# Both halves of P V in one step, one pair of PSUM buffers for four users, and logits scaled as they are copied

## The chip, the core and the metric

The kernel runs on one core of a Trainium2 chip. The metric is device time in microseconds (us) of one execution. TensorE (PE, with its weight loads PEld) multiplies matrices into PSUM; VectorE (DVE), ScalarE (ACT) and GpSimd (POOL) work on PSUM and SBUF; SyncE (SP) issues the DMAs, transposes by DMA among them, in one queue.

## What is computed

The reference chains three layers over batches of 576 positions and 512 channels:

```python
# 1. attention in a window of 64 positions, 8 heads of 64
scores = scale * np.matmul(q, k.transpose(0, 1, 3, 2))
mask = (rel >= 0) & (rel < window)
attn = softmax(np.where(mask, scores, -1000000000.0))
x = np.matmul(attn, v)                       # heads side by side: 512 channels
# 2. gated convolution over 5 positions
gate = 1.0 / (1.0 + np.exp(-gate_pre))       # gate_pre: causal convolution of x
x = gate * (x @ w_val) @ w_out
# 3. four causal attention experts, the best two of each position
logits = x @ w_gate
q, k, v = x @ wq[e], x @ wk[e], x @ wv[e]
ye = softmax(causal(scale * (q @ k.T))) @ v @ wo[e]
out = sum of w[e] * ye over the two experts with the largest logits
```

All eight batches use the same weights; results are float32.

## The kernel before

A batch is cut into five tiles of 128 positions (j = 0 to 4, the last of 64), so there are 40 tiles, numbered 0 to 39. Each goes through the same stages. In the first attention: raw q and k are loaded and transposed on TensorE (qt, L669) into PSUM tile tr and copied out (kT, qT); scores (sp, L726 to L730) go to PSUM tile sc; maximum (L737), exponential (L744), a high and a low half-precision part of P (Phl, the low one is the residual of L282); a DMA transpose makes PT (L765); PV (L794) writes PSUM tile o; VectorE scales the row sums (rc, L799), takes the reciprocal (L802) and writes xn (L809). Then xn is transposed (xt, L829) into tr again and drained to xT and xs; TensorE multiplies with w_val (val, L890 to L892, PSUM pj), VectorE applies the gate (L898) and splits into gs; TensorE makes q and k of the experts (qk, L923 to L925) and v with the logits (v3, L941). VectorE does the routing (L992 to L1030). Scores of the experts (s3, L1073, PSUM sc), softmax, a transpose by DMA (P3T, L1118), y (L1153, PSUM o, drained to ys), the output projection (L1178 to L1180, PSUM pj) and the store follow. Products of full precision are made of three half-precision ones.

Matmuls come in several shapes of the array: 128x128 for most, 128x64 for PV of tiles 1 to 4 of a batch and for y, 64-row ones for scores. PV of a tile comes in two halves of four heads each, two planner operations of 24 matmuls (12 for the first tile of a batch, 24 in one operation for the last). Each half needs the PSUM tile o, which has a single buffer and which y uses too. The tile tr, also with a single buffer, is shared by the raw transposes (two a tile), the xn transposes, a transpose of the batch's scales, and some transposes of weights at the start.

No loop fixes the order of instructions. Every stage of every tile is handed to a planner (`Plan`) with a priority (start of the tile plus `OFF` of its stage), durations, what it reads and writes, and the buffers that it holds (`KIND` names the pool, `BUFS` its number of buffers). `Plan.order` starts operations one after the other by its own table of costs and the buffers that are free; the program is written in that order, so each engine has one fixed sequence. At the start the weights are loaded, converted, multiplied together (w_out with the experts' weights, L471 to L489) and split into wval and wproj, with filler matmuls (L1201) between. The lines that matter here:

```python
KIND = dict(..., o1=("o", 2), xp=("tr", 1), yp=("o", 1), qp=("tr", 2), scp=("tr", 1), ...)
for h in range(NB):                      # NB: 2 halves, 1 for the last tile
    op("pv", n, ..., lambda h=h: pv(h), r=[("PT", n)] + vr, w=[("o1", n, h)])
    chain("xn", n, ("rc", n, h), [rcs, rci], [("o1", n, h)], [])
    op("xn", n, ..., xn(h), ...)
```

Of the kernel before, what the change touches and what calls it, by code (L numbers as in the profile page):

```python
# [22 lines left out]
NEG1 = -1.0e37  # L23
PS = 4096.0

BUFS = dict(raw=5, rv=10, qT=2, kT=2, VA=4, VB=2, Phl=1, PT=1, xn=1, xT=3, xs=2, acc=2, ctmp=2, gs=5,
           P3hl=2, P3T=3, V3=7, q3=3, k3=2, ys=2, ot=1, am=2, scs=3, w4=3, sc=2, o=1, tr=1, pj=2,
           w64=3, t1=3, wbig=1, ab=4, wp=1, wcat=1)
KIND = dict(wf=("pj", 1), kT=("kT", 1), k3=("k3", 1), qp=("tr", 2), s1p=("sc", 1), s3p=("sc", 2), o1=("o", 2), xp=("tr", 1), yp=("o", 1),
            scp=("tr", 1), pv=("pj", 1), pq=("pj", 1), pw=("pj", 1), po=("pj", 1), P3hl=("P3hl", 2),  # L30
            P3T=("P3T", 2), wt=("tr", 2), wj=("pj", 2), wc=("sc", 1), wp=("wp", 0), cq=("wp", 0), wcat=("wcat", 0),
            ck=("wcat", 0), cv=("w64", 1))
II = 14109.34
STRETCH = 1.5
OFF = dict(yh=61969.4, x3=76298.1, vl=20442.0, vs=13922.2, qk=54953.8, val=50000.0, ot=20813.6, yn=88307.5, gv=18491.1,
           qt=454.3, qe=-25419.0, gl=26778.7, rt=99733.5, yl=94279.8, s3=67381.4, ex=47180.1, vh=31559.9, st=81376.7,
           xT=10029.4, dq=13818.2, xl=67807.4, am=-5435.3, ph3=58596.7, xn=-25423.0, v3h=38686.3,
           pl=23451.7, o=98000.0, ph=101124.6, pl3=67418.4, h3=52915.4, yt=64737.1, th=53943.5,
           v3l=14936.7, xt=4442.6, l3=40133.4, m3=74450.1, P3T=76142.0, sp=15925.6, ld=59750.6, pv=28118.3,
           vb=7408.6, cv=66570.7)  # L40
SMALL = 70.0
SYNC = dict(PE=200.0, DVE=150.0, ACT=150.0, POOL=100.0, SP=0.0, TQ=0.0, AQ=0.0)
AHEAD = 600.0
# [2 lines left out]
STQ = ("SP",)  # L46
VBQ = ("SP",)
C3Q = ("SP",)
WATV = 23439.39
WATP = 61184.73  # L50
DMA_A = 650.0
DMA_T = 850.0
TCOST = 60.0
QUEUE = 2500.0
BOOST = {0: 49596.2, 3: 463.2, 4: -4467.5, 5: 1761.0, 7: -1392.4, 8: 4527.3}
LD0 = -175524.04
LD1 = 1628.22
ORDER = "raw0 wv0 wv3 wv2 v2 v1 v3 v0 v4 wv1 cw wo2 raw1 wo wo1 raw2 wo0 raw3 wcat raw4 wo3".split()
TENG = "SP"
SWITCH = 93.0  # L60
COLD = 3400.0
# [5 lines left out]
TAIL = 2000.0  # L67
ABSX = -500.0
FILL = 36
EARLY = 2.85  # L70
BIAS = dict(DVE=1500.0, POOL=0.0, ACT=500.0)


# [144 lines left out]
def attention_conv_moe(ctx: ExitStack, tc: tile.TileContext, q, k, v, w_val, conv_w, w_out,  # L218
# [29 lines left out]
    def bank(key, shape, dtype=F32):  # L248
        return new(key, shape, dtype, psum, KIND[key[0]][0])

# [404 lines left out]
    def col(b, i):  # L655
        return T_["sc_d", b][:, i:i + 1]

    def attn1(n):
# [121 lines left out]

        def pv(half):
            pt = T_["PT", n]
            o = bank(("o1", n, half), [128, 4, 66])
            for i in range(4):
                if last:
                    g = ((slice(64 * r, 64 * r + 64), i, 2 * (i % 2 + 2 * (i // 2 ^ r)) + i // 2, T_["VB", n]) for r in (0, 1))
                elif j:
                    g = ((slice(64 * r, 64 * r + 64), 4 * half + i, 2 * i + half, va if r else T_["VB", n]) for r in (0, 1))
                else:
                    g = ((slice(0, 128), 4 * half + i, 2 * i + half, va),)  # L790
                g = tuple(g)
                for a, c in ((0, 0), (0, 1), (1, 0)):
                    for qs, hh, h, vt in g:
                        pe.matmul(o[qs, i, 0:65], lhsT=pt[:, a, hh, qs], rhs=vt[:, c, h, 0:65], start=a + c == 0, stop=a == 1)  # L794
# [14 lines left out]
            ve.tensor_mul(dst, o[:, :, 0:64], rc[:, :, None].to_broadcast([128, 4, 64]))  # L809

        vr = [("VA", n, 0), ("VA", n, 1)] + ([("VB", n)] if j else [])
        for h in range(NB):
            op("pv", n, (("PE", (18 if j else 13) * mm(65)),), lambda h=h: pv(h), r=[("PT", n)] + vr, w=[("o1", n, h)])
            chain("xn", n, ("rc", n, h), [("DVE", lambda h=h: rcs(h)), ("DVE", lambda h=h: rci(h))], [("o1", n, h)], [])
            op("xn", n, (("DVE", dv(256)),), lambda h=h: xn(h),
               r=[("o1", n, h), ("rc", n, h, 1)] + ([("xn", n, 0)] if h else []), w=[("xn", n, h)])
# [93 lines left out]
    def proj(n):  # L910
# [66 lines left out]

        def lg(e):
            w4 = new(("w4", n), [128, 8, E], F32, late())
            copy(e, w4[:, 0], T_["pw", n][:, 128:132])  # L980
        op("v3h", n, both(256, False), v3h,
           r=[("pw", n)], w=[("V3", n, 0)])
        op("v3l", n, (("DVE", dv(256)),), v3l, r=[("pw", n), ("V3", n, 0)], w=[("V3", n, 1)])
        op("v3l", n, both(4, False), lg, r=[("pw", n)], w=[("w4", n, 0)])

        def rtA():

            w4, p = T_["w4", n], T_["pw", n]
            r, raw = rr(), p[:, 128:132]
            other = w4[:, 0][:, None, :].to_broadcast([128, E, E])  # L990
            own = raw[:, :, None].to_broadcast([128, E, E])
            ve.tensor_tensor(r[:, :, 1], other, own, op=OP.is_equal)  # L992
            ve.tensor_tensor(r[:, :, 0], other, own, op=OP.is_gt)
            t = w4[:, 3]
            ve.tensor_reduce(t[:, 0:1], w4[:, 0], axis=AX.X, op=OP.max, negate=True)
            ve.tensor_scalar(t[:, 0:1], t[:, 0:1], col(b, 3), None, op0=OP.mult)

        def rr():
            return T_["pw", n][:, 288:320].rearrange("p (e i f) -> p e i f", e=E, i=2)
# [5 lines left out]

        def rtC():
            w4 = T_["w4", n]
            ac.activation(w4[:, 1], w4[:, 0], AF.Exp, bias=w4[:, 3, 0:1], scale=col(b, 3))

        def rtF():  # L1010
            w4 = T_["w4", n]
# [16 lines left out]
        def rtI():  # L1028
            w4 = T_["w4", n]
            ve.tensor_scalar(w4[:, 4], T_["pw", n][:, 264:268], w4[:, 3, 2:3], None, op0=OP.mult)  # L1030
        op("rt", n, (("DVE", 450.0),), rtA, r=[("pw", n), ("w4", n, 0), ("scs", b, 3)], w=[("pw", n, "c"), ("w4", n, 1)])
        op("rt", n, (("ACT", 190.0),), rtC, r=[("w4", n, 1)], w=[("w4", n, 2)])
        op("rt", n, (("DVE", 300.0),), rtB, r=[("pw", n, "c")], w=[("pw", n, "s")])
        op("rt", n, (("DVE", 250.0),), rtF, r=[("pw", n, "s"), ("w4", n, 2)], w=[("w4", n, 3)])
# [5 lines left out]
    def attn2(n):  # L1040
# [99 lines left out]

        def y():

            o = bank(("yp", n), [128, 2, 128])
            for c in range(2):
                for kt in range(nt):
                    K = rows(kt)
                    v3 = V3[(n0 + kt) % len(V3)]
                    for a, d in ((0, 0), (0, 1), (1, 0)):
                        for r in (0, 1):
                            e = 2 * c + r  # L1150
                            g, x = [(g, es.index(e)) for g, es in enumerate(groups) if e in es][0]
                            i, qs = (kt, slice(64 * x, 64 * x + 64)) if last else (x * nt + kt, slice(0, 128))
                            pe.matmul(o[64 * r:64 * r + 64, c, :T], lhsT=v3[:K, d, e], rhs=T_["P3T", n, g][:K, a * wt // 128 + i, qs],  # L1153
                                      start=c + kt + a + d == 0, stop=c == 1 and kt == j and a == 1)
# [1 line left out]
           [("V3", m, i) for m in range(n0, n + 1) for i in (0, 1)], w=[("yp", n)])  # L1156

        def yh(e):
            copy(e, new(("ys", n), [128, 2, 2, 128], F16, late())[:, 0, :, :T], T_["yp", n][:, :, :T], 1.0 / PS)
        op("yh", n, both(2 * T, False), yh, r=[("yp", n)], w=[("ys", n, 0)])  # L1160

        def yl():
            ys = T_["ys", n]
            residual(ys[:, 1, :, :T], T_["yp", n][:, :, :T], ys[:, 0, :, :T], 1.0 / PS)
        op("yl", n, (("DVE", dv(2 * T)),), yl, r=[("yp", n), ("ys", n, 0)], w=[("ys", n, 1)])

        def o_():
# [70 lines left out]
```

## Time and profile before

| | before |
|---|---|
| device time, median of 3 runs (lowest to highest) | 679.75 us (679.58 to 681.16) |
| device time of the profiled execution | 679.55 us |
| its span, first to last instruction | 677.7 us |
| TensorE busy | 628.5 us (93%) |
| VectorE busy | 557.4 us (82%) |
| ScalarE busy | 515.6 us (76%) |
| GpSimd busy | 483.1 us (71%) |
| mean granted TensorE clock | 0.985 |

The profiled execution and the median of the three runs differ by 0.2 us. "Busy" is the time that an engine executes; matmuls overlap in the array, so a busy TensorE can still lose time between two starts. [...] A wait in the trace is a stretch in which an engine stood still, with the work that ended it.

### The profile page before, as it was taken

To read this page: it belongs to the slowest core of one execution; us is meant where nothing else is said; L and a number is where in the kernel's file an instruction comes from. 1 tells how busy PE (TensorE), PEld (TensorE's weight loads), DVE (VectorE), ACT (ScalarE), POOL (GpSimd) and SP (SyncE) were. 2 spreads that over 40 slices of the span, in tenths; PEclk is the share of its full clock that TensorE was granted. 3 is DMA by queue.
4 is the path that set the end of the run, shared out by engine and by line. 5 is a ranking of instruction groups with operands and counts; after the bars stand their busy time and mean duration, and the time that the engine had idled before them with its cause. 6 is when DMAs were issued, how large, how long until landed. Compare 5 with 4: busy or idle time off the path is not lost. (4 is left out here: it accounts for less than half of the span.)

```text
span 677.7 us, 25338 instructions
## 1 busy us (share of the span) xinstructions
PE 628.5 (93%) x10225; PEld 489.9 (72%) x10237; DVE 557.4 (82%) x1695; ACT 515.6 (76%) x1340; POOL 483.1 (71%) x546
## 2 busy tenths in 40 slices
PE   8979979889999999999989999999999999999985
PEld 4436768677787778777877778777887688767753
DVE  7695697788979988998888886989789898887782
ACT  2656557877897888888797869787897888777773
POOL 4674967997596688786985879497977777973500
PEclk9989989999999999999999999999999999999998
DMA  8769952795995988967996977797686664556257
GB/s 224 188 164 194 235 114 46 163 168 107 157 223 120 173 153 139 196 129 143 162 184 142 180 134 154 156 177 150 114 172 129 96 127 111 98 114 118 43 123 145
DMA packets 306531, 99.45 MB, mean 147 GB/s; under 512 B 294362, under 2 KB 296942, under 8 KB 306414
## 3 DMA queue, kind: packets, MB, share of 16 engines
q1 hardware_dynamic: 306414, 97.84, 74.1%
q8 instruction: 80, 1.31, 0.8%
q14 instruction: 37, 0.30, 0.1%
HBM read 34.63 MB, written 9.44 MB: 65 GB/s over the span
## 5 line engine op out<-in xcount | busy, mean ns | idle before, releaser
L872 POOL TENSOR_TENSOR acc<-acc,ctmp 128x512 f32<-128x512 f32 (+1 forms) x160 | 185.9, 1162 | 6.3
L870 POOL TENSOR_TENSOR ctmp<-xT,cw 128x512 f32<-128x512 f32 (+1 forms) x160 | 151.5, 968 | 0.0
L744 ACT ACTIVATE sc<-sc,mx 128x128 f32<-128x128 f32 x288 | 99.0, 344 | 33.0 <-DVE mx L737 25.0
L890 PE MATMUL pj<-xs,wval 128*128 128x128 f16 (+1 forms) x640 | 101.1, 216 | 1.0 <-ACT k L275 1.0
L923 PE MATMUL pj<-gs,wproj 128*128 128x128 f16 (+1 forms) x640 | 101.6, 216 | 0.1
L924 PE MATMUL pj<-gs,wproj 128*128 128x128 f16 (+1 forms) x640 | 101.4, 216 | 0.0
L925 PE MATMUL pj<-gs,wproj 128*128 128x128 f16 (+1 forms) x640 | 101.4, 216 | 0.0
L891 PE MATMUL pj<-xs,wval 128*128 128x128 f16 (+1 forms) x640 | 101.0, 215 | 0.0
L892 PE MATMUL pj<-xs,wval 128*128 128x128 f16 (+1 forms) x640 | 100.9, 215 | 0.0
L1087 ACT ACTIVATE sc<-sc,mx 128x128 f32<-128x128 f32 (+3 forms) x144 | 75.9, 527 | 30.2 <-DVE mx L1082 27.3
L861 POOL TENSOR_TENSOR acc<-xT,cw 128x512 f32<-128x512 f32 (+1 forms) x31 | 31.7, 1023 | 81.9 <-issue 40.7
L282 DVE SCALAR_TENSOR_TENSOR P3hl<-sc,mx,P3hl 128x128 f16<-128x128 f32 (+3 forms) x144 | 75.8, 573 | 11.6 <-ACT P3hl L275 10.3
L275 ACT ACTIVATE P3hl<-sc,mx 128x256 f16<-128x256 f32 (+4 forms) x134 | 66.4, 564 | 8.9 <-DVE mx L1100 4.9
L1073 PE MATMUL sc<-k,q 64*128 64x128 f32 (+5 forms) x384 | 66.5, 451 | 4.9 <-DVE P3hl L282 3.5
L1082 DVE TENSOR_REDUCE mx<-sc 128x4 f32<-128x512 f32 (+3 forms) x64 | 61.5, 965 | 3.4 <-PE sc L1073 2.6
L923 PEld LDWEIGHTS <-wproj 128*128 128x128 f16 x640 | 62.1, 99 | 2.3 <-issue 0.5
L890 PEld LDWEIGHTS <-wval 128*128 128x128 f16 x640 | 61.9, 99 | 1.7 <-issue 0.9
L891 PEld LDWEIGHTS <-wval 128*128 128x128 f16 x640 | 61.9, 99 | 1.6 <-issue 1.1
L924 PEld LDWEIGHTS <-wproj 128*128 128x128 f16 x640 | 62.1, 99 | 0.5 <-issue 0.3
L925 PEld LDWEIGHTS <-wproj 128*128 128x128 f16 x640 | 62.1, 99 | 0.0
L892 PEld LDWEIGHTS <-wval 128*128 128x128 f16 x640 | 61.9, 99 | 0.0
L691 POOL TENSOR_TENSOR VA<-rv,VA 128x512 f16<-128x512 f32 (+1 forms) x40 | 45.9, 1156 | 19.5 <-ACT VA L275 11.4
(200 smaller groups left out, 1763.4 us busy)
## 6 DMA issues: line engine op xcount, KB each, us to landing
VB<-VA SPq DMA_DIRECT2D x64, 132.0 KB, 2.9
raw<-in_q SPq DMA_DIRECT2D x32, 256.0 KB, 3.9
raw<-in_k SPq DMA_DIRECT2D x32, 256.0 KB, 3.8
rv<-in_v SPq DMA_DIRECT2D x32, 256.0 KB, 3.9
out<-ot SPq DMA_DIRECT2D x32, 256.0 KB, 2.7
w<-in_moe_w_val SPq DMA_DIRECT2D x4, 512.0 KB, 5.2
w<-in_moe_w_out SPq DMA_DIRECT2D x4, 512.0 KB, 3.7
rv<-in_v SPq DMA_DIRECT2D x8, 128.0 KB, 3.5
```

The lines of the kernel that those rows point to most:

```text
L282: ve.scalar_tensor_tensor(o, i, scale, hi, op0=OP.mult, op1=OP.subtract)
L744: ac.activation(ps[:, i, :], ps[:, i, :], AF.Exp, bias=t[:, hh:hh + 1])
L870: po.tensor_mul(y, x[:, :, t + i:t + i + T], W["cw"][:, :, t + i:t + i + 1].to_broadcast([128, 4, T]))
L872: po.tensor_add(acc[:, :, :T], acc[:, :, :T], y)
L890: pe.matmul(p[:, m, :T], lhsT=w0, rhs=xs[:, 0, c, :T], start=c == 0, stop=False)
L891: pe.matmul(p[:, m, :T], lhsT=w0, rhs=xs[:, 1, c, :T], start=False, stop=False)
L892: pe.matmul(p[:, m, :T], lhsT=w1, rhs=xs[:, 0, c, :T], start=False, stop=c == 3)
L923: pe.matmul(p[:, m, :T], lhsT=w0, rhs=gs[:, 0, c, :T], start=c == 0, stop=False)
L924: pe.matmul(p[:, m, :T], lhsT=w0, rhs=gs[:, 1, c, :T], start=False, stop=False)
L925: pe.matmul(p[:, m, :T], lhsT=w1, rhs=gs[:, 0, c, :T], start=False, stop=c == 3)
L1073: pe.matmul(ps[ot, c0:c0 + r.shape[-1]], lhsT=l, rhs=r, start=bk not in seen, stop=i == final[bk])
L1087: ac.activation(ps[:, x], ps[:, x], AF.Exp, bias=mx[:, x:x + 1], accum_out=mx[:, 4 + x:5 + x])
```

## The change

PV of both halves becomes one planner operation, so that its 48 matmuls (24 for the first tile of a batch) stand in a row; the chains of rc and xn follow for both halves. Its two results, y, the raw and xn transposes and the transpose of the scales all use the PSUM tile tr, which now has two buffers; the tile o is gone. The PSUM tiles of PV and y are declared as large as a buffer and used in part. The copy of the logits out of PSUM multiplies them by the batch's scale, so that the maximum needs no scaling of its own and the exponential no scale; the two compares of the routing scale the other operand as they read it. xn gets a second buffer, v's raw tile rv nine instead of ten. The planner's tables (priorities, order of loads, and constants) have new values throughout, so the order changes on all engines.

```diff
-BUFS = dict(raw=5, rv=10, ..., xn=1, ..., sc=2, o=1, tr=1, pj=2,
+BUFS = dict(raw=5, rv=9, ..., xn=2, ..., sc=2, tr=2, pj=2,
-KIND = dict(..., o1=("o", 2), xp=("tr", 1), yp=("o", 1),
+KIND = dict(..., o1=("tr", 2), xp=("tr", 1), yp=("tr", 1),
-OFF = dict(yh=61969.4, x3=76298.1, vl=20442.0, vs=13922.2, qk=54953.8, val=50000.0, ot=20813.6, yn=88307.5, gv=18491.1,
+OFF = dict(yh=34829.2, x3=87092.4, vl=19158.9, vs=12206.5, qk=54953.8, val=50000.0, ot=19786.5, yn=88113.8, gv=18985.3,
...
-ORDER = "raw0 wv0 wv3 wv2 v2 v1 v3 v0 v4 wv1 cw wo2 raw1 wo wo1 raw2 wo0 raw3 wcat raw4 wo3".split()
+ORDER = "wv0 wv2 wv3 v4 raw0 v1 v3 v2 wv1 raw1 wo2 cw v0 raw2 wo3 raw3 wo wo1 wcat wo0 raw4".split()
...
-            o = bank(("o1", n, half), [128, 4, 66])
+            o = bank(("o1", n, half), [128, 512])[:, 0:264].rearrange("p (i d) -> p i d", d=66)
+            T_["o1", n, half] = o
...
+        def pvs():
+            for h in range(NB):
+                pv(h)
+        op("pv", n, (("PE", (18 if j else 13) * mm(65) * NB),), pvs, r=[("PT", n)] + vr, w=[("o1", n, h) for h in range(NB)])
         for h in range(NB):
-            op("pv", n, (("PE", (18 if j else 13) * mm(65)),), lambda h=h: pv(h), r=[("PT", n)] + vr, w=[("o1", n, h)])
...
-            copy(e, w4[:, 0], T_["pw", n][:, 128:132])
+            copy(e, w4[:, 0], T_["pw", n][:, 128:132], col(b, 3))
...
-            ve.tensor_tensor(r[:, :, 1], other, own, op=OP.is_equal)
-            ve.tensor_tensor(r[:, :, 0], other, own, op=OP.is_gt)
-            t = w4[:, 3]
-            ve.tensor_reduce(t[:, 0:1], w4[:, 0], axis=AX.X, op=OP.max, negate=True)
-            ve.tensor_scalar(t[:, 0:1], t[:, 0:1], col(b, 3), None, op0=OP.mult)
+
+            ve.scalar_tensor_tensor(r[:, :, 1], own, col(b, 3), other, op0=OP.mult, op1=OP.is_equal)
+            ve.scalar_tensor_tensor(r[:, :, 0], own, col(b, 3), other, op0=OP.mult, op1=OP.is_lt)
+            ve.tensor_reduce(w4[:, 3, 0:1], w4[:, 0], axis=AX.X, op=OP.max, negate=True)
...
-            ac.activation(w4[:, 1], w4[:, 0], AF.Exp, bias=w4[:, 3, 0:1], scale=col(b, 3))
+            ac.activation(w4[:, 1], w4[:, 0], AF.Exp, bias=w4[:, 3, 0:1])
...
-            o = bank(("yp", n), [128, 2, 128])
+            o = bank(("yp", n), [128, 4, 128])
```

How the order moves shows at three places. The first is VectorE in the middle of the program, in the last rows ahead of the residual of P of tile 23 (Phl). Names before the arrow are written, those behind it read; rc and xn belong to PV of tile 22, in the rows of before to its second half (the first half's stand ahead of these rows). Before:

```order
L1030 TENSOR_SCALAR w_7848<-pj,w_7848 128x4
L898 SCALAR_TENSOR_TENSOR pj<-acc,pj 128x512
L799 TENSOR_SCALAR rc<-o 128x4
L1096 TENSOR_SCALAR mx_8005<-mx_8005,w_7848 128x1
L802 RECIPROCAL rc<-rc 128x4
L1096 TENSOR_SCALAR mx_8005<-mx_8005,w_7848 128x1
L809 TENSOR_TENSOR xn<-o,rc 128x4x64
L1100 RECIPROCAL mx_8005<-mx_8005 128x2
L282 SCALAR_TENSOR_TENSOR Phl<-sc,Phl 128x1024
```

and in the changed kernel:

```order
L902 SCALAR_TENSOR_TENSOR pj<-acc,pj 128x512
L1033 TENSOR_SCALAR w_7803<-pj,w_7803 128x4
L800 TENSOR_SCALAR rc<-tr 128x4 x2
L803 RECIPROCAL rc<-rc 128x4 x2
L1099 TENSOR_SCALAR mx_7881<-mx_7881,w_7803 128x1
L810 TENSOR_TENSOR xn<-tr,rc 128x4x64
L911 TENSOR_TENSOR gs<-pj,gs 128x512
L810 TENSOR_TENSOR xn<-tr,rc 128x4x64
L1099 TENSOR_SCALAR mx_7881<-mx_7881,w_7803 128x1
L282 SCALAR_TENSOR_TENSOR Phl<-sc,Phl 128x1024
```

Both halves' rc and xn now stand together ahead of the residual, and the split into gs has come ahead of it too.

The second is TensorE from the scores of tile 23 (L730) to the next y (L1153, in the changed kernel L1156); the PV that stands there is tile 22's. Of each operation its first or last row is shown. Before:

```order
L730 MATMUL sc<-kT,qT 64x128 x16
...
L794 MATMUL o<-VB,PT 64x65
...
L1073 MATMUL sc<-k_6374,q_7574 128x512 x2
...
L669 MATMUL tr<-ident,raw 128x128 x4
...
L892 MATMUL pj<-xs,wval 128x128
...
L794 MATMUL o<-VB,PT 64x65
...
L1178 MATMUL pj<-wo_133,ys 128x512
...
L829 MATMUL tr<-ident,xn 128x128 x4
...
L1153 MATMUL o<-P3T,V_1_107 64x128
```

and in the changed kernel:

```order
L730 MATMUL sc<-kT,qT 64x128 x16
L1076 MATMUL sc<-k_6454,q_7520 128x512 x2
...
L669 MATMUL tr<-ident,raw 128x128 x4
...
L896 MATMUL pj<-xs,wval 128x128
...
L795 MATMUL tr<-VA_104,PT 64x65
...
L1183 MATMUL pj<-wo_133,ys 128x512
...
L1156 MATMUL tr<-P3T,V_1_107 64x128
```

The first half of PV has moved from behind the scores to the second half's place, and y has come ahead of the transposes of xn.

The third is TensorE near the start, around the first transposes of w_out (L471, of the converted weight t) and the first product of weights (L489); L728 and L730 are scores, L520 a transpose of a maximum, the rows on band_first are fillers. Before:

```order
L669 MATMUL tr<-ident,raw 128x128 x4
...
L730 MATMUL sc<-kT,qT 64x128 x16
L471 MATMUL tr<-ident,t_455 128x128 x4
...
L1201 MATMUL pj<-band_first,identb 128x512
L520 MATMUL tr<-ident,cm 1x128
L489 MATMUL pj<-wcat,wbig 128x512 x4
```

and in the changed kernel:

```order
L730 MATMUL sc<-kT,qT 64x128 x16
L669 MATMUL tr<-ident,raw 128x128 x4
...
L1204 MATMUL pj<-band_first,identb 128x512
L471 MATMUL tr<-ident,t_455 128x128 x4
...
L1204 MATMUL pj<-band_first,identb 128x512
L520 MATMUL tr<-ident,cm 1x128
L489 MATMUL pj<-wcat,wbig 128x512 x4
L471 MATMUL tr<-ident,t_528 128x128 x4
```

A raw transpose and six fillers now stand between the scores and the w_out transposes.

## Rows read from the trace of the kernel before

**Rows 1.** Busy time by stretch; PE, PEld, DVE, ACT, POOL, clock, DMA share, GB/s.
```profile
0.00:50.00 50.00, 41.01 (x251) 21.50 (x256) 39.08 (x73) 24.40 (x49) 30.42 (x43) 0.97 0.77 196
50.00:130.00 80.00, 72.55 (x893) 56.87 (x894) 57.98 (x154) 53.97 (x128) 58.40 (x55) 0.96 0.66 145
130.00:650.00 520.00, 496.68 (x8822) 401.26 (x8827) 446.20 (x1419) 423.89 (x1133) 393.77 (x446) 1.00 0.77 144
```

**Rows 2.** Waits of TensorE, 0 to 130 us: total, times, longest (us).
```profile
PE o L794 <- DVE xn L809: 4.0, 1, 4.0
...
PE tr L471 <- DVE kT L277: 3.0, 1, 3.0
PE tr L669 <- DVE cw L422: 1.6, 1, 1.6
```

**Rows 3.** Waits of TensorE, 130 to 650 us.
```profile
PE o L794 <- DMA PT<-Phl: 5.4, 5, 2.5
...
PE tr L669 <- DVE xs L842: 1.4, 2, 0.9
...
PE tr L829 <- ACT kT L275: 0.7, 1, 0.7
PE tr L669 <- ACT kT L275: 0.6, 1, 0.6
...
PE o L794 <- DVE xn L809: 0.6, 2, 0.4
```

**Rows 4.** Timeline of TensorE around three halves of PV: start, duration (us), work.
```profile
303.55 0.38 PE L1178 MATMUL pj<-wo,ys 128*128 128x512 f16 x1
...
304.41 0.38 PE L1179 MATMUL pj<-wo,ys 128*128 128x512 f16 x1
304.63 0.38 PE L1180 MATMUL pj<-wo,ys 128*128 128x512 f16 x1
304.94 0.22 PE L794 MATMUL o<-VB,PT 128*64 128x65 f16 x1
...
305.31 0.20 PE L794 MATMUL o<-VA,PT 128*64 128x65 f16 x1
305.34 0.34 PE L954 MATMUL pj<-wproj,gs 128*64 128x132 f16 x6
...
316.33 0.20 PE L794 MATMUL o<-VA,PT 128*64 128x65 f16 x1
316.46 0.33 PE L669 MATMUL tr<-ident,raw 128*128 128x128 f32 x1
```

**Rows 5.** Timeline of VectorE ahead of the first qk.
```profile
92.86 3.93 DVE L282 SCALAR_TENSOR_TENSOR wproj<-wp,sp,wproj 128x1024 f16<-128x1024 f32 x3
96.71 0.15 DVE L799 TENSOR_SCALAR rc<-o 128x4 f32<-128x4 f32 x1
...
98.82 0.41 DVE L809 TENSOR_TENSOR xn<-o,rc 128x256 f32<-128x256 f32 x1
99.15 1.25 DVE L282 SCALAR_TENSOR_TENSOR wproj<-wp,sp,wproj 128x16 f16<-128x16 f32 x1
```

**Rows 6.** Timeline of VectorE for P of tile 23.
```profile
373.50 1.21 DVE L737 TENSOR_REDUCE mx<-sc 128x8 f32<-128x1024 f32 x1
...
380.16 1.23 DVE L282 SCALAR_TENSOR_TENSOR Phl<-sc,Phl 128x1024 f16<-128x1024 f32 x1 [0.30 <-ACT Phl L275]
```

**Rows 7.** Timeline of SyncE's queue and of TensorE for the same tile.
```profile
381.69 2.97 SPq L765 DMA_TRANSPOSE PT<-Phl  x1
...
386.73 0.50 PE L730 MATMUL sc<-kT,qT 64*64 64x128 f32 x12
388.26 0.22 PE L794 MATMUL o<-VB,PT 128*64 128x65 f16 x1 [1.03 <-DMA PT<-Phl]
```

**Rows 8.** The tile PT: time of its transposes from issue to landing.
```profile
DMA to landing us min/median/max: 2.4/4.4/7.0
```

**Rows 9.** VectorE's group of line L996: count, then busy us and mean ns.
```profile
L996 DVE TENSOR_SCALAR w<-w,sc_d 128x1 f32<-128x1 f32 x40 | 8.6, 214 | 1.4
```

## What I predicted, and from what

> **What bounds the kernel now.** I read the busy time by stretch first [rows 1]. From 130 to 650 us TensorE is busy 496.68 of 520 us; VectorE is busy 446.20, ScalarE 423.89. So the middle is bound by TensorE's own work plus 23.3 us in which it stands still. The head (0 to 130 us) leaves it 16.4 us of standing still. Next I read the waits of TensorE, first of the head [rows 2], then of the middle [rows 3]. In the middle the longest is PV waiting for the transposed P (PT, 5.4 us in 5 waits); waits of one PSUM user for the drain of the user ahead of it (tr L669 and L829 for xs and kT, o L794 for xn) are 1.4 + 0.7 + 0.6 + 0.6 = 3.3 us. Last I read matmul starts one by one where the shape of the array changes [rows 4], because no wait shows there: it is inside "busy".
>
> **The change part by part.**
>
> *PV in one piece (TensorE).* A half is 24 matmuls of 128x64, two at a time. Its neighbours are mostly 128x128. [rows 4] price the change of shape. Inside an output projection starts stand 0.22 us apart (304.41, 304.63), but the first PV matmul comes 0.31 us after the last of them (304.94): 0.09 us. At the end, the last PV start is 0.13 us ahead of a 128x128 transpose (316.33, 316.46), but 0.03 us ahead of a matmul of the same 128x64 shape (305.31, 305.34): 0.10 us. I take 0.095 us a change of shape. Three of a batch's five tiles have two such halves, 24 tiles in all, so at most 48 changes go. Counted along TensorE's order, before has 307 changes of shape and the changed kernel 261: 46 fewer, 46 x 0.095 = **4.4 us** of TensorE's own time, which nothing hides. This is the one firm term.
>
> [...]
>
> *One pair of PSUM buffers.* Before, tr (raw transposes, xn transposes, scales) has one buffer, o (PV, y) another. Now all take turns on two, and PV takes both at once. In the middle the waits by which this can gain are the 3.3 us above; it can also lose, since behind a merged PV both buffers are held until VectorE has made xn of both halves. I take half, **1.7 us** gained (from 3.3 gained to the loss in the last rival).
>
> *The head.* Two waits of [rows 2] are waits for the one tr buffer: 3.0 us, in which the transposes of w_out stand behind kT's copy on VectorE, and 1.6 us for the copy of cw. With two buffers, and with six filler matmuls and a raw transpose put ahead (the last pair of orders), they can go; but the fillers are no work, and if the weights arrive no earlier nothing is won. Between 0 and 4.6 I take half, **2.3 us**. The 4.0 us behind xn I leave where they are: [rows 5] show that xn waits on VectorE behind 3.93 us of wproj residuals, and the next useful matmul, qk, needs the last of these (99.15 + 1.25). Merged or not, TensorE has to wait for it. The order of loads changes too, with the same transfers ahead of the weights of qk; I cost that at nothing, and at 3 us either way for the range.
>
> *VectorE's order around PV.* Take tile 23, [rows 6 to 8]. Its scores are reduced from 373.50, the residual of P ends at 380.16 + 1.23 = 381.39, the transpose is issued at 381.69, and PV starts at 388.26, 6.6 us later, after 1.03 us of standing still. So TensorE was there 13.7 us after 373.50. In the new order tile 24's scores (ending 387.23, about 0.7 us) stand behind this PV instead of ahead, one pair of shape changes is gone (0.2) and small gaps of 0.4 us may close: TensorE is there after 12.4 us. On VectorE the xn chains of tile 22 stand ahead of the residual in both orders; the split into gs now does too, and some routing no longer does (first pair of orders). I cost that at nothing. So PT lands as before, 14.8 us after 373.50, and TensorE waits 2.4 instead of 1.0 us. With a landing after 4.4 us, the median of [rows 8], it waits 0.2. Three tiles stand exactly so (18, 23, 28), three more (8, 13, 33) with over 1.4 us more between. I price this at 3 x (-0.8 to +1.4), from 2.4 us gained to 4.2 lost, and take **1.5 us lost**, nearer to what the row of this very tile shows.
>
> *Logits scaled in their copy.* This takes one VectorE instruction off each of 40 tiles, 8.6 us in all [rows 9], and makes two compares three-operand ones of the same size. VectorE is not the bound, and routing runs 20 us and more ahead of the P that needs it; TensorE covers it: nothing. If VectorE were the bound it would give up to 8.6 us. A second xn buffer and nine instead of ten v buffers: nothing, since v is loaded over two tiles ahead.
>
> *The tail.* The order moves, the same chain stays (scores, softmax, transpose, y, projection, store): nothing, 2 us either way.
>
> Sum, against the profiled execution's 679.55 us (its span is 677.7; the median of the three runs is 0.2 us above it): 679.55 - 4.4 - 1.7 - 2.3 + 1.5 = 672.65, **672.7 us**.
>
> **The rivals.**
>
> *All waits go.* Two buffers end the 3.3 us in the middle and the 4.6 us of the head, and PT is ready in time (2.4 us gained): 679.55 - 4.4 - 3.3 - 4.6 - 2.4 = 664.9 us. For it: the new order repeats evenly batch by batch. Against it: waits that vanish usually show the next one.
>
> *The gain is given back at PT.* The head and the buffers win nothing, and the transposes land late: 679.55 - 4.4 + 4.2 = 679.4 us, no change. For it: PT is already the longest wait in the middle, and TensorE arrives sooner.
>
> *The pair of buffers becomes the bound: slower.* After each of the 32 merged PVs, VectorE must run two reciprocal chains and two xn before the buffers are free, and y stands behind one output projection only in two tiles of five. That projection takes 1.4 us (303.55 to 304.94, [rows 4]); the chain for the first buffer is two scalings of 0.15, two reciprocals of about as much and one xn of 0.41 [rows 5], 1.0 us if VectorE is free. VectorE is busy 86% of the middle, so often something of 0.7 to 1.2 us is ahead: TensorE waits up to 0.8 us. At all 32 that is 25.6 us at the most; at half of them 12.8. Without the gain from the buffers the other terms leave 4.4 + 2.3 - 1.5 = 5.2 us, so the change turns slower where the wait after a merged PV exceeds 5.2 / 32 = 0.16 us on average. At half of the 32: 679.55 - 5.2 + 12.8 = 687.2 us.
>
> [...]
>
> *It doesn't do what it says.* The order already shows the merged PV with no row between its halves; the 46 changes of shape are counted from it. I give that nothing.
>
> **How the numbers follow.** Forecast 672.7 (667 to 677.5): 0.56. All waits go, 664.9: 0.18. Given back at PT, 679.4: 0.12. Pair of buffers, 687.2: 0.14. About 0.3% (2 us) is what a measurement of this kernel can tell from no change, so faster means under 677.7 and slower above 681.8. Faster 0.56 + 0.18 = 0.74, same 0.12, slower 0.14. The range leaves out a tenth at either end: it cuts into the first rival at 664 and takes in the given-back case and the lighter part of the last rival, up to 682.
>
> **What would show it.** Right: TensorE's busy time falls by 4 to 5 us with as many matmuls; no wait of L795 for xn in the middle; the head's wait of the w_out transposes for kT is gone, and the wait of the first qk for wproj is there in its place. PV of tiles 18, 23 and 28 would wait for PT for 0 to 2.5 us. Wrong: rows of tr waiting for xn, rc or ys that sum to over 5 us, busy time that does not fall, a granted clock below 1.00 in the middle, or a first qk later than its 100 us.

## The result, and the profile after

| | before | after |
|---|---|---|
| device time, median | 679.66 us | 669.35 us (4 executions, 666.92 to 671.88) |
| ratio, 95% interval | | 0.986 (0.982 to 0.990) |
| the same kernel again, beside other executions of before | 679.24 us | 671.66 us (6 executions); 0.988 (0.985 to 0.991) |
| profiled execution, its span | 679.55, 677.7 us | 671.88, 670.1 us |
| TensorE busy | 628.5 us | 623.7 us |
| VectorE, ScalarE, GpSimd busy | 557.4, 515.6, 483.1 us | 554.8, 510.0, 487.1 us |

The change makes the kernel faster by 8 to 10 us; 672.7 was forecast. Busy time by stretch of the kernel after, the rows that answer to [rows 1] (TensorE, its weight loads, VectorE, ScalarE, GpSimd, granted clock, DMA share, GB/s):

```profile
0.00:50.00 50.00, 45.57 (x281) 24.74 (x282) 35.67 (x72) 24.78 (x49) 27.24 (x39) 1.00 0.77 206
50.00:130.00 80.00, 73.08 (x987) 59.01 (x986) 63.45 (x164) 56.77 (x140) 66.12 (x64) 0.96 0.68 151
130.00:650.00 520.00, 493.28 (x8824) 397.27 (x8823) 448.97 (x1410) 422.70 (x1123) 393.24 (x444) 1.00 0.74 143
```

In the first 50 us TensorE stands still for 4.4 us and not 9.0, at a granted clock of 1.00 and not 0.97. In the middle it stands still for 26.7 us and not 23.3: it has less to do there, and what it saved is not all in the time. Its waits in the middle, which answer to [rows 3] (total, times, longest):

```profile
PE tr L1156 <- DMA P3T<-P3hl: 3.8, 3, 2.1
PE sc L1076 <- DVE Phl L282: 2.8, 3, 1.3
PE tr L833 <- DVE mx L1099: 2.6, 1, 2.6
PE tr L795 <- DMA PT<-Phl: 2.6, 2, 1.4
...
PE tr L833 <- DVE xn L810: 0.4, 2, 0.2
```

PV's waits for PT fell from 5.4 to 2.6 us, waits for xn are next to nothing, and in their place stand waits for P3T, for the scores' buffer (Phl) and for one mx.

Fixed times mislead here, since the kernel after is ahead. So I cut both traces where TensorE has done a tenth, a fifth and nine tenths of its useful matmul work (columns by passes, fillers left out):

| share of the work | before | after | after, repeated | difference (after) |
|---|---|---|---|---|
| 0 to 10% | 79.8 us | 72.8 us | 72.9 us | -7.0 us |
| 10 to 20% | 73.1 us | 72.9 us | 74.8 us | -0.2 us |
| 20 to 90% | 450.3 us | 444.5 us | 444.9 us | -5.8 us |
| 90% to the end | 74.5 us | 79.9 us | 78.9 us | +5.4 us |

The sum of the last column is the 7.6 us by which the spans differ. The head gave most, the middle something, and the tail lost. The 20 to 90% stretch, of before, then of after (busy time by stretch):

```profile
152.90:603.20 450.30, 433.07 (x7687) 349.96 (x7691) 389.42 (x1245) 371.86 (x988) 349.58 (x391) 1.00 0.78 147
```

```profile
145.70:590.20 444.50, 427.47 (x7750) 347.14 (x7746) 387.73 (x1199) 368.31 (x973) 356.56 (x398) 1.00 0.77 150
```

TensorE's work there is 5.6 us less and its standing still is the same, 17.2 and 17.0 us.

### The profile page after: what moved, and what is told of

Its sections match the earlier page's. It is cut to its first block, busy times and chain, and to the rows that moved or that the text cites. A ratio compares the mean times of both kernels' runs of the same rounds, so it can differ in the third digit from the quotient of the medians.

```text
span 670.1 us, 25290 instructions
## 1 busy us (share of the span) xinstructions
PE 623.7 (93%) x10237; PEld 487.4 (73%) x10237; DVE 554.8 (83%) x1663; ACT 510.0 (76%) x1320; POOL 487.1 (73%) x549
## 5 line engine op out<-in xcount | busy, mean ns | idle before, releaser
L865 POOL TENSOR_TENSOR acc<-xT,cw 128x512 f32<-128x512 f32 (+1 forms) x34 | 34.4, 1011 | 71.2 <-issue 36.0
L275 ACT ACTIVATE P3hl<-sc,mx 128x256 f16<-128x256 f32 (+4 forms) x143 | 69.4, 559 | 9.8 <-DVE mx L1103 3.7
```

Source lines behind the costliest of these rows:

```text
L275: ac.activation(o, i, AF.Copy, scale=scale)
```

## Experiments

Three kinds: small edits of the changed kernel that leave its order alone (sw1, sw3, logits); kernels that the planner orders anew; and edits of the kernel before with its order held fixed by a list in the planner's place. The stretch from 20 to 90% of the work is what they are compared by in the middle:

| kernel | median, ratio to before (95%) | 20 to 90% | TensorE busy in it | standing still |
|---|---|---|---|---|
| before | 679.2 to 679.7 | 450.3 us | 433.1 us | 17.2 us |
| after; repeated | 669.35; 671.66 | 444.5; 444.9 | 427.5; 428.5 | 17.0; 16.4 |
| sw1 | 676.66, 0.994 (0.992 to 0.997) | 444.4 | 430.0 | 14.4 |
| sw3 | 672.56, 0.989 (0.986 to 0.993) | 448.3 | 438.3 | 10.0 |
| logits | 670.84, 0.988 (0.984 to 0.992) | 444.9 | 426.9 | 18.0 |
| split | 683.46, 1.005 (1.003 to 1.008) | 454.2 | 430.0 | 24.2 |
| structure_only | 692.67, 1.020 (1.016 to 1.024) | 461.2 | 430.3 | 30.9 |
| tables_only | 705.26, 1.037 (1.034 to 1.040) | 467.0 | 437.4 | 29.6 |
| pair | 682.41, 1.003 (1.000 to 1.005) | 451.9 | 434.0 | 17.9 |
| merged | 701.27, 1.031 (1.028 to 1.034) | 465.6 | 433.7 | 31.9 |

Each row of the last three columns is one trace. Busy time lies between 427 and 438 us; the standing still, from 10 to 32 us, differs more. The granted clock of the stretch is 0.99 in split, tables_only, pair and merged, and 1.00 in the others.

### The price of a change of shape: sw1 and sw3

```diff
+            full = bank(("o1", n, half), [128, 512])
+            o = full[:, 0:264].rearrange("p (i d) -> p i d", d=66)
             for i in range(4):
+                if 0 < j < NT - 1 and (half, i) in BREAK:      # sw1: {(1, 0)}; sw3: {(0, 2), (1, 0), (1, 2)}
+                    pe.matmul(full[:, 300:304], lhsT=identb, rhs=identb[:, 0:4], start=True, stop=True)
```

> The changed kernel with one small matmul of 128x128 (4 columns, into columns that nobody reads) put between the two halves of the merged PV, in the 24 tiles whose halves are 128x64. The order of everything else is the same, so 48 changes of the array's shape come back and nothing moves. Theory (a change of shape costs 0.095 us of TensorE's own time, which nothing hides): 24 x (2 x 0.095 + about 0.03 for the matmul itself) = 5.3 us, so 669.35 + 5.3 = 674.6 us, and a busy time 4 to 5 us longer. Rival (waits set TensorE's pace, so that the gain of the change is not from changes of shape): within 1.5 us of 669.35.

> As the run with one small matmul, but with three of them in each of the 24 tiles: 72 matmuls and 144 changes of shape. Theory: 72 x 0.22 = 15.8 us, 685.2 us, three times what one gives. Rival (waits set the pace): 0 to 3 us, 669 to 672 us. Between the two, the share that waits take up is read from the slope between one and three.

The small matmul (L789) in the timeline of TensorE of sw1 (start, duration, work):

```profile
305.01 0.20 PE L799 MATMUL tr<-VA,PT 128*64 128x65 f16 x1
305.14 0.18 PE L789 MATMUL tr<-identb 128*128 128x4 bf16 x1
305.25 0.22 PE L799 MATMUL tr<-VB,PT 128*64 128x65 f16 x1
```

From one PV start to the next lie 0.24 us, at this place and at all 24 (and at all 72 of sw3), where two pairs of PV otherwise start 0.03 us apart: 0.21 us more for a small matmul with its two changes of shape, as the 0.22 of the expectation. The price of [rows 4] holds. The middle stretch of sw1, then of sw3:

```profile
144.80:589.20 444.40, 429.97 (x7763) 350.34 (x7765) 388.38 (x1202) 367.39 (x971) 355.23 (x397) 1.00 0.77 150
```

```profile
146.00:594.30 448.30, 438.26 (x7800) 356.51 (x7802) 389.35 (x1199) 368.45 (x971) 354.81 (x396) 1.00 0.77 148
```

All of it runs at a granted clock of 1.00, the highest in these traces, in sw1, sw3 and the kernel after. TensorE has 2.5 and 10.8 us more to do than in the kernel after, and the stretch takes 0.1 us less and 3.8 us more: its waits shrink from 17.0 to 14.4 and to 10.0 us. In these traces the first 2.5 us cost nothing, and of 10.8 us a third shows. sw3 took 672.56 us in all, 0.9 to 3.2 us above the two measurements of the kernel after, where 15.8 us more were forecast. So TensorE's work is real time, but other chains arrive at nearly the same moment and take up part of what it saves or loses.

The median of sw1 does not fit this: 676.66 us, above sw3 with three times the matmuls, and 5.0 to 7.3 us above the kernel after, where the theory gave 5.3. The trace of sw1 is that of its fastest execution, 672.0 us at a mean granted clock of 0.990; most of its others stand at 0.981. If the clock falls to 0.50 there, as in before from 46.40 to 49.80 us, that is (0.990 - 0.981) x 2 x 670 = 12 us more at 0.50, up to 6 us lost by a busy TensorE, an estimate from these numbers and about the difference within sw1. It does not explain the difference from the kernel after: executions of that at 0.980 to 0.983 took 671.8 to 673.2 us, executions of sw1 at 0.981 to 0.983 took 676.3 to 677.9. Where in the program sw1 loses these 4 to 5 us, no trace here shows. By whole times, then, one small matmul costs about what the theory says and three cost less than one. sw3 shows that waits hide a part of added work; that a little work is free, the middle of one trace shows and the whole times do not.

### The logits: logits

```diff
-            copy(e, w4[:, 0], T_["pw", n][:, 128:132], col(b, 3))
+            copy(e, w4[:, 0], T_["pw", n][:, 128:132])
...
+            ve.tensor_scalar(t[:, 0:1], t[:, 0:1], col(b, 3), None, op0=OP.mult)
```

> The changed kernel with only the edit of the logits undone: raw copy, a scaling instruction of its own (40 more on VectorE, 8.6 us of busy time), scale in the exponential, two-operand compares. The tables stay those of the change. Theory (VectorE isn't the bound, routing is far ahead of its users): 669.35 us, within 1 us. Rival (VectorE's queue sets the middle): up to 8.6 us more, 678 us; half of that if VectorE sets half of it, 673.7 us.

Measured 670.84 us, between the two measurements of the kernel after, and the middle the same to 0.4 us. The edit of the logits is worth nothing that can be measured, as forecast.

### Structure and tables apart, ordered anew: again, tables_only, structure_only, split

again is the kernel after. tables_only is before with the new numbers (`OFF`, `WATV`, `WATP`, `BOOST`, `LD0`, `LD1`, `ORDER`, `EARLY`), structure_only is after with the old ones, split is after with

```diff
-        op("pv", n, ..., pvs, r=[("PT", n)] + vr, w=[("o1", n, h) for h in range(NB)])
         for h in range(NB):
+            op("pv", n, ..., lambda h=h: pv(h), r=[("PT", n)] + vr, w=[("o1", n, h)])
```

> The changed kernel once more, unaltered, beside the kernels sent with it, since its first comparison rests on four executions. If the first comparison holds: a ratio of 0.982 to 0.990 to before, 667 to 672 us. If the four executions were lucky: 0.990 or above, 673 us and more, and then one small matmul between the halves, at 676.7 us, would have cost half of what it seemed to.

> The kernel before with the tables of the change alone (priorities, order of loads, constants); PV in two halves, tile o and tile tr with one buffer each, logits as before. 303 changes of shape against 307 of before and 261 of the change. Theory (the tables are worth nothing without the pair of buffers and the merged PV): 679.7 us within 3 us. Rival (the tables are what wins, through the order of loads and priorities): 669 to 673 us. If the structure is what wins and the tables are fitted to it: above 681 us.

> The changed kernel with the tables of before: merged PV, one pair of PSUM buffers, logits scaled in their copy, with the old priorities and order of loads. 275 changes of shape, 32 fewer than before. Theory (shape changes 3.0 us, the head's waits for the one buffer up to 4.6 us, the buffer waits of the middle 1.7 us): 679.7 - 3.0 - 2.3 - 1.7 = 672.7 us. Rival (only the tables make a use of the structure): 679.7 us within 3 us, or slower.

> The changed kernel with PV as two operations of the planner again, one for each half, on the shared pair of PSUM buffers and with the tables of the change; the planner may put other work between the halves. Theory (the merging itself is worth its changes of shape, 4.4 us): 673.8 us, less what the earlier release of the first half's buffer gives back (under 1 us). Rival (a merged PV holds both buffers and so costs waits that the halves don't have): 669 us or below. Rival (the tables of the change fit a merged PV alone): over 676 us, with new waits of TensorE.

The repeat agrees with the first comparison. The structure alone is 13 us slower than before, the tables alone 26 us: the theory failed for structure_only, whose rival holds (only the tables make a use of the structure), and of tables_only the last case holds, tables that are fitted to the structure. Of split the last rival holds too. split has about as many changes of shape as the kernel after (259 against 261), since the new order puts the halves beside one another or beside y; it is 12 us slower than the repeat all the same, so changes of shape are not what it lost. TensorE's waits in the middle of split and of structure_only:

```profile
PE tr L795 <- DMA PT<-Phl: 5.6, 5, 1.9
PE sc L1076 <- DVE Phl L282: 5.6, 5, 3.5
PE sc L1076 <- DVE P3hl L282: 4.2, 7, 1.3
```

```profile
PE tr L669 <- ACT qT L275: 3.9, 3, 1.9
PE tr L669 <- DVE xs L846: 3.3, 1, 3.3
PE sc L728 <- DVE P3hl L282: 2.7, 4, 0.9
PE tr L669 <- DVE ys L282: 2.5, 2, 2.2
```

In split it is the longest chains (PT, scores) that come late, in structure_only the raw transposes that stand behind drains of the shared pair (qT, xs, ys). The structure wants an order that is fitted to it; the tables are fitted to this structure.

### One part alone at the old order: pair and merged

pair changes `KIND` and `BUFS` of the kernel before (and the declared sizes of PV's and y's tiles), and the order of all instructions stays:

```diff
-           ..., sc=2, o=1, tr=1, pj=2,
+           ..., sc=2, tr=2, pj=2,
-KIND = dict(..., o1=("o", 2), xp=("tr", 1), yp=("o", 1), ...
+KIND = dict(..., o1=("tr", 2), xp=("tr", 1), yp=("tr", 1), ...
```

merged is pair with the list altered: PV's first half stands ahead of its second, and its rc and xn follow behind both.

> The kernel before in its own order, held fixed instruction by instruction (a list takes the planner's place), with one thing altered: the tiles o and tr become one pair of PSUM buffers. PV stays in two halves, 307 changes of shape as before. Theory (one user's wait for the drain of another is what the pair ends): the head loses 2.3 to 6.3 us (4.6 us of waits and the clock's fall behind them), the middle up to 3.3 us: 670 to 676 us. Rival (what moves the time is the order, not the buffers): within 1.5 us of 679.2. Rival (sharing makes users wait that had a buffer of their own): above 681 us.

> As the run with the pair of buffers in the order of before, and PV's first half moved to the place of the second, with its rc and xn right behind; nothing else moves. 268 changes of shape, 39 fewer. Theory (a change of shape is TensorE's own time and nothing hides it): 39 x 0.095 = 3.7 us below the run with the pair alone. Rival (waits take up what TensorE saves, as they took up what small matmuls added between 20 and 90% of the work): no more than 1 us below it. Rival (merged PV holds both buffers, and xn of both halves comes late): above it.

The pair of buffers by itself wins nothing. Its 682.41 us would by the number bear out the last rival, but its executions at a granted clock of 0.984 and above took 677.9 to 679.4 us, as before does, so that a loss is not shown either. In the middle TensorE stands still for 17.9 us. In the head the w_out transposes (L471) no longer wait and come at 39.93 us, not 45.72, but the wait for kT is still there, now in front of the transpose of cm, and the first product of weights then waits for wbig. TensorE's wait and starts, and ScalarE ahead of them, in pair:

```profile
PE tr L520 <- DVE kT L277: 3.3, 1, 3.3
```

```profile
39.93 0.75 PE L471 MATMUL tr<-ident,t 128*128 128x128 f32 x4
...
46.45 6.08 PE L489 MATMUL pj<-wcat,wbig 128*128 128x512 f32 x8 [1.41 <-ACT wbig L275]
```

```profile
42.92 2.96 ACT L744 ACTIVATE sc<-sc,mx 128x128 f32<-128x128 f32 x8 [5.23 <-DVE mx L737]
45.81 0.59 ACT L275 ACTIVATE wbig<-tr 128x512 f32<-128x512 f32 x1
```

The copy of wbig stands behind exponentials on ScalarE that wait for a maximum on VectorE. So the first product comes at 46.45 us, against 47.65 before, and 0.95 us of this only because the whole execution starts that much earlier (VectorE copies cw at 36.18 and not 37.13 us).

And with PV merged at the old order the kernel loses 19 us more. Waits of TensorE in the middle of merged:

```profile
PE tr L669 <- DVE xn L810: 4.5, 7, 1.1
...
PE tr L830 <- DVE xn L810: 3.2, 5, 1.0
...
PE tr L795 <- DVE xn L810: 2.8, 3, 0.9
```

Here is the rival of the prediction in which the pair of buffers becomes the bound: 10.5 us of waits for xn by three users of the pair, against 1.1 us in pair and 0.4 us in the kernel after. Two things differ between merged and the kernel after in the middle, the logits' edit and v's tenth buffer aside: the order, and a second buffer for xn, which merged lacks. structure_only has that buffer and the old tables and is 21 us slower than the repeat, which speaks for the order as the larger part; what the buffer does by itself was not tried. In the new order rc and xn of both halves stand together behind PV on VectorE, and on TensorE the scores, val or an output projection mostly stand between PV and the next user of the pair.

### The head: weights_in_o, weights_in_o_fixed, v_later

```diff
-            wt=("tr", 2),
+            wt=("o", 2),
```

> The kernel before with one thing altered: the transposes of the weights at the start go into the PSUM tile o (which has nothing to do there) and not into tr, so that they no longer stand behind the raw transposes' copies. Theory (two users of one buffer cost the head 3.0 + 1.6 us of waiting and, with the clock that falls behind them, 1.7 us more): first product of weights 4 to 6 us earlier, the clock at 1.00 up to 90 us, 674 to 676 us in all. Rival (the weights arrive no earlier than they are used): first product where it is, 47.7 us, and 679.7 us in all. The planner orders the program anew, so that the middle may move by 2 us either way; the head is read from the trace.

> The kernel before in its own order, held fixed, with the weights' transposes of the start in the PSUM tile o and not in tr; nothing else is altered and nothing moves. Theory (two users of one buffer cost the head its 3.0 us wait of the w_out transposes for kT, and the 1.6 us wait of a raw transpose for cw): first product of weights 3 to 5 us earlier than 47.7 us, no fall of the clock at 46 us, and 674 to 677 us in all. Rival (behind these waits the weights or the converted t come late as well): first product within 1 us of 47.7 us, and 679.2 us.

Both theories fell. Ordered anew, the kernel lost 17 us (696.11, ratio 1.025), at the old order 9 us (688.17, 1.011). With buffers of their own the transposes of weights still wait, first in weights_in_o_fixed, then in weights_in_o:

```profile
PE o L520 <- DVE t L374: 5.2, 1, 5.2
...
PE o L471 <- DVE xn L810: 3.6, 2, 2.0
```

```profile
PE o L520 <- DVE cm L515: 6.0, 1, 6.0
```

In weights_in_o TensorE waits for cm, a maximum that VectorE finds late. In weights_in_o_fixed the row names a conversion of VectorE that ends at the same moment, but what L520 needs is the tile o, and this is emptied by the same copy of wbig as in pair, again behind the exponentials (45.49 + 0.59 us); its first product comes at 46.30 us, no earlier than the 1.3 us by which the whole execution is ahead. Later TensorE waits for PV's drain in the tile o. The wait for kT of [rows 2] was a wait for VectorE's queue, and the one buffer only gave it a name. What makes the queue late stands in VectorE's and GpSimd's timelines of before:

```profile
33.79 3.42 DVE L374 SCALAR_TENSOR_TENSOR t<-w,t 128x512 int32<-128x512 int32 x1
...
37.22 5.49 DVE L282 SCALAR_TENSOR_TENSOR wval<-wbig,sv,wval 128x512 f16<-128x512 f32 x4
```

```profile
34.03 2.03 POOL L687 TENSOR_TENSOR rv<-rv,sc_s 128x512 f32<-128x512 f32 x2
...
39.07 3.09 POOL L691 TENSOR_TENSOR VA<-rv,VA 128x512 f16<-128x512 f32 x2
```

and of after:

```profile
33.60 0.69 DVE L374 SCALAR_TENSOR_TENSOR t<-w,t 128x512 int32<-128x512 int32 x1
```

```profile
36.57 2.33 POOL L387 TENSOR_SCALAR w<-w 128x512 f32<-128x512 f32 x1 [5.38 <-ACT w L379]
```

One conversion takes 3.42 us beside GpSimd's work on v and 0.69 where GpSimd stands still for 5.38 us. v_later tests it at the old order:

```diff
-  GpSimd: ... L687 x2 (rv, tiles 2, 3), L691 x2 (VA), L687 (rv, tile 4), L387, L388 (t), L387, L388 (t), ...
+  GpSimd: ... L387, L388 (t), L387, L388 (t), L687 x2, L691 x2, L687, ...
```

> The kernel before in its own order, held fixed, with one thing moved: five GpSimd operations at the start (scaling and low half of v of tiles 2 to 4, L687 and L691), which run from 34.0 to 43.6 us beside VectorE's conversion of a weight (L374, 3.42 us) and the low half of wval (L282, 5.5 us), go behind the conversions of w_out; two copies of ScalarE that read them go along. In the changed kernel GpSimd stands still there, and the same VectorE instructions take 0.69 and 2.9 us. Theory (these two-input instructions of VectorE are held up by GpSimd's, and that, not the single buffer, is the head's wait for kT): L374 at 34 us takes 0.7 to 1.5 us, wval's four 3 to 4 us, the w_out transposes come 2 to 3 us earlier than 45.7 us and so does the first product. Rival (VectorE is slow there for another reason, such as the transfers that arrive): L374 stays over 3 us and the first product at 47.7 us. All in all 676 to 680 us, since GpSimd's own work comes about 2 us later behind it; a repeat of before gave 679.4.

VectorE, then TensorE's first product of weights, in v_later:

```profile
32.42 0.83 DVE L374 SCALAR_TENSOR_TENSOR t<-w,t 128x512 int32<-128x512 int32 x1
33.18 0.17 DVE L422 COPY cw<-tr 128x20 f32<-128x20 f32 x1
33.27 3.11 DVE L282 SCALAR_TENSOR_TENSOR wval<-wbig,sv,wval 128x512 f16<-128x512 f32 x4
```

```profile
41.18 3.67 PE L489 MATMUL pj<-wcat,wbig 128*128 128x512 f32 x8
```

In before the first product stood here:

```profile
47.65 4.67 PE L489 MATMUL pj<-wcat,wbig 128*128 128x512 f32 x8
```

The conversion takes 0.83 us, wval 3.11, the wait for kT is gone, and the first product comes at 41.18 us and not 47.65 (1.4 us of it because this whole execution starts that much earlier), which is more than the 2 to 3 us forecast. The theory holds: GpSimd's work on v held these instructions of VectorE up (the conversion 3.42 us beside it, 0.83 without it; wval 5.49 and 3.11), and that made the head late. By what mechanism, no run shows. The two copies of ScalarE that moved along are not the reason: in the kernel after, copies of ScalarE (wval, 32.21 to 34.16 us) run beside the conversion of 0.69 us. Not every GpSimd instruction costs so much; this one of v_later stands beside wval, which takes 0.2 us more than in the kernel after (3.11 against 2.9):

```profile
34.30 1.79 POOL L387 TENSOR_SCALAR w<-w 128x512 f32<-128x512 f32 x1 [1.59 <-ACT w L379]
```

All in all v_later took 680.47 us, ratio 1.001 (0.999 to 1.004), just above the 676 to 680 forecast: the gain is given back at once. A wait of TensorE and what stood ahead of it on ScalarE, in v_later:

```profile
PE tr L471 <- ACT wbig L275: 5.8, 1, 5.8
```

```profile
50.33 0.63 ACT L275 ACTIVATE VA<-rv 128x512 f16<-128x512 f32 x1 [3.62 <-POOL rv L687]
```

The copies of v that went along stand ahead of wbig's copy on ScalarE and wait for GpSimd. That is this edit's own fault; in the kernel after, the copies move too and nothing waits behind them.

## Why the prediction was right

The time lies 3.3 us (1.0 in the repeat) from the forecast and inside its range, on the side that was given 0.74. But the sum came out by errors that cancel, so that it came so near is luck.

| step of the sum | forecast | measured | |
|---|---|---|---|
| changes of shape | -4.4 | price of one as read (sw1); TensorE busy -4.8 over the whole run, with 12 matmul rows more in it | "nothing hides it" wrong |
| buffers in the middle | -1.7 | 0 (pair: standing still 17.9 against 17.2) | wrong |
| PT of tiles 18, 23, 28 | +1.5 | these three +0.4 (0, 1.03, 1.11 us of waits to 1.41, 0, 1.17); PT in all 5.4 to 2.6, so -2.8 | too large, and the other tiles left out |
| these three, 10 to 90% | -4.6 | -6.0 (-3.7 in the repeat) | |
| head | -2.3 | -7.0 | mis-sized, wrong cause |
| logits | 0 | 0 | right |
| tail | 0, 2 either way | +5.4 (+4.4 in the repeat) | wrong |

**Changes of shape.** The 0.095 us was read rightly: the matmul put between the halves costs 0.21 us as a start interval. But the step "nothing hides it" fails. In sw3, of 10.8 us that TensorE has more to do in the middle 3.8 show, the rest is taken up by waits that shrink, and merged, with 39 changes fewer, stands still for 14 us more than pair. (sw1 is divided: nothing in the middle of its trace, about the full price in its whole time.) From before to after TensorE's work fell by 5.6 us in the middle while its standing still stayed at 17 us. pair, merged and structure_only speak for the order as what kept it there; which part of the 5.8 us the shape changes own by themselves stays open.

**Buffers in the middle.** The waits that I priced (xs, kT, xn: 3.3 us) shrank to 0.8 (xn 0.4, kT 0.4), and others took their place. pair shows that the buffers alone win nothing. The loss that I set against them is real at the old order, 10.5 us of waits for xn in merged, and was escaped by the new one. I treated the order of VectorE around PV as a detail with a cost of nothing; it decides the sign.

**PT.** I kept the 14.8 us from the scores to the landing of PT and let TensorE come sooner. Tiles 18 and 28 wait inside the 0 to 2.5 us that I gave and tile 23 not at all, but the longest wait of before, 2.5 us, stood at another tile and is gone.

**Head.** The two waits of [rows 2] went, and the clock's fall behind them too, so the gain lies above the upper end that I gave, 4.6 us. The stretch of the fall in the kernel before, at a granted 0.50 (busy time by stretch), which costs a busy TensorE about half of its 3.4 us, an estimate from the 0.50 (the row of eight products that begins in it takes 4.67 us, and 3.70 in the kernel after at a granted 1.00):

```profile
46.40:49.80 3.40, 3.25 (x7) 1.40 (x6) 3.30 (x7) 2.66 (x8) 1.72 (x2) 0.50 0.47 104
```

At the order of before the cause was not the single buffer (pair, weights_in_o_fixed) but VectorE held up by GpSimd (v_later, the conversion 0.83 us and not 3.42); in the kernel after the new order of loads and priorities puts the work on v later, and its first product comes 5.0 us earlier than the 47.65 of before:

```profile
42.61 3.70 PE L489 MATMUL pj<-wcat,wbig 128*128 128x512 f32 x8
```

The tables without the pair do not give this, nor the pair without the tables. In tables_only the conversion takes 0.69 us too, but with one tr buffer TensorE waits for cw (first row) and the first product comes at 49.43 us; in structure_only the conversion takes 5.50 us (second fence), and the first product comes at 51.43 us. What the pair adds in the new order was not tried by itself.

```profile
PE tr L669 <- DVE cw L422: 3.9, 1, 3.9
```

```profile
33.26 5.50 DVE L374 SCALAR_TENSOR_TENSOR t<-w,t 128x512 int32<-128x512 int32 x1
```

I read which tile a wait named, and not what the releasing engine was busy with. The step on the 4.0 us behind xn failed too: the first qk does not wait for wproj but starts at 92.56 and not at 100.09 us, with waits of 1.9 and 1.1 us ahead of it.

**Tail.** I wrote that the same chain stays. It does, but it comes later: TensorE's waits for P3T from 90% of the work on, before (first row) and after (second fence):

```profile
PE o L1153 <- DMA P3T<-P3hl: 1.9, 2, 1.4
```

```profile
PE tr L1156 <- DMA P3T<-P3hl: 5.3, 5, 2.1
```

In the repeat they are 7.1 us. In the last 22 us of the kernel after the granted clock is 0.71, against 0.85 before:

```profile
648.00:670.10 22.10, 12.61 (x155) 6.66 (x153) 8.46 (x23) 7.74 (x17) 0.47 (x4) 0.71 0.62 130
```

In the last 21.5 us of the repeat the clock is 0.83, and its tail is still 4.4 us longer than before, so the clock is not the main part. The new order runs the experts' chain of the last tiles later, as the waits for P3T show, and I had not looked at it.

**The rivals.** "All waits go" was wrong: standing still stays at 17 us. "Given back at PT" was wrong in place, though something was given back, in the tail. The pair as a bound is right for the old order alone. From 20 to 90% the granted clock of the kernel after is 1.00 with four users on one pair; in the repeat it falls once, to 0.51 from 203.6 to 207.0 us, right behind a single wait of 2.3 us (L833 for mx), and the kernel after waits 2.6 us at that place without a fall.

## What to carry to other kernels

A wait names the last thing that was late; before it is priced, look at what the releasing engine did in the microseconds ahead, and whether its own instructions took longer than the same ones elsewhere. In a kernel whose order is planned, a change of buffers or of grouping has no price of its own: the same structure gave 670 us with tables fitted to it and 693 us with the old ones, and nearly the same (merged) 701 us at the old order, so reckon with the order, and look at head, middle and tail apart. When engines are nearly balanced (TensorE 95% busy, VectorE 86%), saved or added work of the busiest is worth its time only as far as the waits behind it don't fill in, and one trace of a kernel is not enough to tell a few us.

## What the runs showed of the hardware

A conversion on VectorE (L374, 128x512) took 0.69 us while GpSimd stood still (after), 3.42 us beside GpSimd's work on 128x512 tiles (before) and 0.83 us with its work on v moved away (v_later); one of 5.50 us stands in structure_only. One low half of wval took 0.74 us (after, four in 2.9) and 1.37 us beside GpSimd (before, four in 5.49). A change of TensorE's array shape cost 0.09 us from 128x128 to 128x64 and 0.10 us back ([rows 4]), and a matmul of 4 columns with its two changes 0.21 us (sw1). Executions of one program differed by up to 7 us (before, in one set of 22: 676.1 to 683.2 us), mostly along with their granted clock (sw1: 0.990 at 672.0 us, 0.981 at 676.7 us).
